# A fused scan and feed-forward kernel: the small scan products of the first two groups in fewer places, no filler products, one rounding step earlier

## The chip, the core and the metric

The kernel runs on one core of one Trainium2 chip. A core has TensorE (PE; its weight loads are shown as PEld), VectorE (DVE), ScalarE (ACT), GpSimd (POOL) and SyncE (SP, which here only issues transfers). Each works through its own queue in the order in which the program was written, and the engines wait for each other through semaphores. The metric is the device time of one execution in microseconds (us), less being better. The kernel before the change takes 375.94 us, the median of three runs (375.88 to 376.27). Its profile is of one more execution: 376.32 us by the same clock, and 374.6 us from the first to the last instruction, which is the span that all positions below count from.

## The reference

Two stages follow each other. The first is a Mamba-2 scan over 4 batches, 8 heads and 768 positions, head size 32, state size 16, cut into chunks. The reference uses chunks of 32; the result does not depend on the chunk.

```
la    = log(clip(a, 1e-6, 1));  cum = cumsum(la) within the chunk
M     = (C B^T) * exp(cum_i - cum_j) for i >= j, else 0
y     = M x  +  (C state) * exp(cum)
state = exp(sum la) * state + sum_j exp(cum_last - cum_j) B_j x_j
```

The second stage takes y as 3072 tokens of 256 numbers and computes `h = y w_in` (256x2048), `g = h * sigmoid(1.702 h)` and `g w_out` (2048x256). The weights come as 64-bit floats, and the kernel turns them into 32-bit ones on the chip.

## The kernel before, in words

**Tiling.** The kernel works with chunks of 128 positions. A batch has 6 chunks, so there are 24 in all, taken as 12 pairs (p = 0 to 11). A group is 512 tokens: two pairs, six groups (g = 0 to 5). For each group the scan of its two pairs gives yT, and the feed-forward follows in 8 blocks (j) of two hidden slices each.

**The scan of one pair** is a row of small products on TensorE, each of which uses the 128x128 array cut into strips: `turn_only` transposes B and C into one bank (tp), and ScalarE copies it out as BT and CT (L496). `gain` forms the state increments (A, L567, strips of 32 columns), and `keep` puts them into the state on VectorE. `score` forms C times B (cb, L539, strips of 32 rows), `weigh` multiplies it with the decay matrix L on VectorE (L550), and `since_start` scales C by the decay since the chunk's start (CsT, L524). `finish` forms y from state and L (L603, L612), and ScalarE copies the two halves of y into yT (L634). For the later pairs the decay matrix is made by a VectorE scan over broadcast rows of a (`decay`, L347). Pair 2 gets it from `fan_all`: four products (ab2, L355) spread rows of a over the array, and VectorE scans them (L382). `since_fanned` does the same for the decay since the start of the later chunks of batch 0, from two small products (L422 and L436).

**The start.** Pairs 0 and 1 are made from exponentials of differences. `mask` products (L447) preset the banks, `differ` adds the differences of the cumulated logarithms (L455), and ScalarE takes exponentials (L474). Ahead of `differ` stand one `keep_busy` product, six masks that are used, and two masks into a bank `idle` that nobody reads.

**The weights** come in ten pieces. For each, `fields` (L157, L160) splits the words on VectorE, `clamp` limits the exponent with two ScalarE instructions (L168, L169), `rounded` adds the low word (L173, VectorE), and `join` (L184, L190, VectorE) writes the piece into w_in or w_out. `narrow(i)` is `rounded(i)`, `fields(i+1)`, `join(i)`.

**The dense products.** Group 0 makes all its hidden slices first (`half`, `hidden`, L668 and L654) and then runs `project_all`, which accumulates 16 slices f into two banks (o, L766). Group 1 makes its hidden slices (steps H0 to H7) interleaved with the second product in a seven-product scheme (steps P0 to P7, `product`, L823). From group 2 on the first product uses a seven-product scheme too (`first`, L726 and L736). These schemes need mixed operands, which VectorE makes: `mix_in`, `mix_w`, `mix_y`, `mix_g`.

**What sets the order.** The order is written out by hand: tables `in_hidden`, `in_project` and `after` say what small work is put behind or ahead of which slice or step, and strings of steps do it for the later groups. At the end `in_order` fixes each engine's order as it was recorded. In `in_hidden[0]` the work stands behind slice f; in `in_project[0]` ahead of it; in `after` behind the named step.

**Banks.** Small results and hidden slices share a pool of four accumulation banks (`bank`, pool ps). An area of four more banks (`area`, pool psa) holds ab, cb or acc in turn. A tile of a pool waits until the last reader of the bank that it gets is done.

Of the kernel before, what the change touches and what calls it, by code (L numbers as in the profile page):

```python
# [16 lines left out]
P = 128  # L17
# [18 lines left out]
def kernel(  # L36
# [126 lines left out]
    def clamp(i):  # L163


        e = power[i]
        z = e.bitcast(FP32)
        nc.scalar.activation(z, e, AF.Relu, scale=-8.0, bias=edge[:, 0:1])  # L168
        nc.scalar.activation(e, z, AF.Relu, scale=-1.0, bias=edge[:, 1:2])  # L169
# [182 lines left out]
    def fan(p, r, ab):  # L352

        rows = slice(32 * r, 32 * r + 32)
        nc.tensor.matmul(out=ab, lhsT=ones[rows], rhs=fans[p][rows].rearrange("p k q i -> p (k q i)"),  # L355
                         start=True, stop=True, tile_position=(32 * r, 0),
                         skip_group_check=True)

    def fan_all(p):

        ab = area(f"ab{p}")
        for r in range(R):
            fan(p, r, ab[:, r])
        for r in range(R):
            decay_heads(p, r, ab[:, r])
        for k in range(2):
            ends(p, k)
# [51 lines left out]
    def fan_rows(t, c0, c1):  # L419

        o = bank(f"rows{c0}")[:, :(c1 - c0) * P]
        nc.tensor.matmul(out=o, lhsT=whose.rearrange("p h n -> p (h n)"),  # L422
                         rhs=t[:32, c0:c1].rearrange("p c s -> p (c s)"), start=True,
                         stop=True, tile_position=(0, 0), skip_group_check=True)
        return o
# [4 lines left out]
        nc.scalar.activation(since[0][:, :CG].rearrange("p c s -> p (c s)"),  # L430
                             fan_rows(cum, 0, CG), AF.Exp)

    def since_fanned():

        t, f = fan_rows(az, CG, NC), bank("starts")[:, :NC - CG]
        nc.tensor.matmul(out=f, lhsT=whose.rearrange("p h n -> p (h n)"),  # L436
                         rhs=starts[1][:32, CG:, 0], start=True, stop=True,
                         tile_position=(0, 0), skip_group_check=True)
        first = ssd.tile([P, NC, P], FP32, tag="first", name="first0", bufs=1)[:, CG:]
        nc.gpsimd.memset(first, 0.0)  # L440
        nc.vector.tensor_copy(first[:, :, 0], f)
        nc.vector.tensor_tensor_scan(
            out=since[0][:, CG:].rearrange("p c s -> p (c s)"), data0=t,
            data1=first.rearrange("p c s -> p (c s)"), initial=0.0, op0=ALU.mult, op1=ALU.add)

    def mask(t):
        nc.tensor.matmul(out=t, lhsT=identb, rhs=below.unsqueeze(1).to_broadcast([P, 4, P]),  # L447
                         start=True, stop=False, skip_group_check=True)
# [31 lines left out]
    def bank(name):  # L480
        return ps.tile([P, 4 * P], FP32, tag="ff", name=name)
# [448 lines left out]
    for r in range(2):  # L930
        ab[1, r] = bank(f"ab1_{r}")
        mask(ab[1, r])
    idle = bank("idle")
    for i in range(2):
        mask(idle)
    differ(0, [(r, ab[0, r]) for r in range(R)])
    exps(0, range(R))
    nc.vector.tensor_copy(idents, ident.unsqueeze(1).to_broadcast([P, NH, P]))
# [1 line left out]
    since_exp()  # L940
    fields(0)
    clamp(0)
    score(0, ab0)
    differ(1, [(r, ab[1, r]) for r in range(2)])
    exps(1, range(2))
# [1 line left out]
    ends(0, 0, nc.gpsimd)  # L947
    ends(0, 1, nc.gpsimd)
    weigh(0)
    rounded(0)  # L950
    turn_only(1, ("ACT", "ACT", "ACT"))
    gain(0)
    for r in range(2, R):
# [45 lines left out]
    at(in_hidden[0], 8, lambda: pick_a(PG))  # L999
    at(in_hidden[0], 9, lambda: clamp(6))  # L1000
    at(in_hidden[0], 9, lambda: fan_all(PG))
    at(in_hidden[0], 11, since_fanned, lambda: narrow(6))
    at(in_hidden[0], 15, lambda: clamp(7))
    for k in range(2):
        at(in_hidden[0], 5 + k, lambda k=k: spread(CG + 2 + k))
    at(in_hidden[0], 6, lambda: load(PG + 1))
    at(in_project[0], 0, lambda: turn_only(PG), lambda: narrow(7), lambda: since_start(PG))
    at(in_project[0], 1, lambda: advance(PG), lambda: clamp(8), lambda: decay(CG + 2))
    at(in_project[0], 4, lambda: scores(PG), lambda: narrow(8))
    at(in_project[0], 6, lambda: finish(PG), lambda: clamp(9), lambda: decay(CG + 3),  # L1010
       lambda: clip_rows(1), lambda: decay_rows(1))
    at(in_project[0], 7, lambda: turn(PG + 1))
    at(in_project[0], 9, lambda: narrow(9))
    at(in_project[0], 10, lambda: advance(PG + 1), lambda: scores(PG + 1))
    at(in_project[0], 14, lambda: finish(PG + 1))
    for i in range(4):
        at(in_project[0], 14, lambda i=i: mix_in(i))
    for k in range(PG):
# [3 lines left out]


    after = {}
    n, p = 2 * PG, 3 * PG

    def late(p):
        gain(p)
# [1 line left out]
        score(p)  # L1030
        weigh(p)

    at(after, "H0", lambda: decay(2 * CG), lambda: decay(2 * CG + 1), lambda: turn(n))
    at(after, "H1", lambda: late(n), lambda: decay(2 * CG + 2), lambda: decay(2 * CG + 3),
       lambda: turn(n + 1))
    at(after, "H3", lambda: finish(n), lambda: load(p + 1), lambda: late(n + 1))
    at(after, "H4", lambda: finish(n + 1))
    for k, i in enumerate(("H4", "P0", "P2", "P5")):
        at(after, i, lambda k=k: mix_w(k))
    for j in range(NF // 2):  # L1040
        at(after, f"P{min(j - 1, 5)}" if j else "H4", lambda j=j: mix_g(1, j))
    for k in range(CG):
        at(after, f"P{k}", lambda k=k: decay(3 * CG + k))
        at(after, "H1" if k < 2 else "H3", lambda k=k: spread(3 * CG + k))
    at(after, "P3", lambda: clip_rows(2), lambda: decay_rows(2), lambda: turn(p))
    at(after, "P4", lambda: mix_y(2), lambda: advance(p), lambda: turn(p + 1))
    at(after, "P5", lambda: advance(p + 1))
    assert [b for b in range(NB) if 3 * CG <= b * NC < 4 * CG] == [2]


# [7 lines left out]
    project_all(0, in_project[0])  # L1058
    load(p)
    spread_rows(2)  # L1060
    for step in "H0 H1 H2 H3 H4 P0 H5 P1 H6 P2 H7 P3 P4 P5".split():
        j = int(step[1:])
        if step[0] == "H":
            hidden(1, 2 * j)
            hidden(1, 2 * j + 1)
        else:
            product(1, j)
        for do in after.get(step, []):
            do()
# [14 lines left out]

    def seven(g, j):
        return [(g, j, (i,)) for i in ORDER]

    for g in range(2, NG):
        n, p = (g + 1) * PG, (g + 2) * PG
        more, most = g + 1 < NG, g + 2 < NG  # L1090
        chunks = list(range((g + 2) * CG, (g + 3) * CG)) if most else []
        rows = [b for b in range(NB) if most and (g + 2) * CG <= b * NC < (g + 3) * CG]
        if most:
            load(p)
            for c in chunks[:2]:
                spread(c)
            for b in rows:
                spread_rows(b)
        run(g, "0.1 P P 0.6 P P 0.7 P 0.5 P 0.2 P 0.D", seven(g - 1, 6))
        run(g, "1.1 0.S P 0.4 P P 1.6 P 0.3 0.T M P P 1.7 P 1.5 1.2 1.D C", seven(g - 1, 7),  # L1100
            M=lambda: mix_g(g, 0), C=lambda: combine(g - 1))
        def along():
            for r in rows:
                clip_rows(r)
                decay_rows(r)

        def refill():
            if most:
                load(p + 1)
                for c in chunks[2:]:  # L1110
                    spread(c)

        if more:

            run(g, "2.1 1.S 1.4 1.3 2.6 2.5 2.2 2.7 1.T s1 2.D 2.S w1 give 2.4 3.1 2.3 3.5 2.T 3.6 "
                "s2 w2 y1 refill 3.7 3.2 3.D along 4.1 P P 3.4 P 3.S 4.6 P 3.3 4.5 3.T M1 P P y2 4.7 P 4.2 4.D M2",
                seven(g, 0), s1=lambda: score(n), w1=lambda: weigh(n), give=lambda: give(g - 1),
                s2=lambda: score(n + 1), w2=lambda: weigh(n + 1), y1=lambda: finish(n),
                refill=refill, along=along, y2=lambda: finish(n + 1), M1=lambda: mix_g(g, 1),
                M2=lambda: mix_g(g, 2))  # L1120
            if most:
                decay(chunks[0])
        else:
            run(g, "2.1 1.S 1.4 1.3 2.6 2.5 2.2 2.7 1.T 2.D 3.1 2.S 2.4 3.5 3.6 2.3 3.2 3.7 2.T 3.D M",
                M=lambda: mix_g(g, 1))
        for j in range(5 if more else 4, NF // 2):
            h = "{1}.1 {0}.S P {0}.4 P {1}.6 P {0}.3 P {1}.7 {0}.T P {1}.5 P {1}.2 P {1}.D M".format(j - 1, j)
            run(g, h, seven(g, j - 4), M=lambda: mix_g(g, j - 2))
            if most:
                decay(chunks[j - 4])  # L1130
        k = NF // 2 - 1
        run(g, f"P {k}.S P {k}.4 P P {k}.3 {k}.T P P P", seven(g, 4))
        if not more:
            give(g - 1)
            for j in range(k - 1, k + 1):
                mix_g(g, j)
            break
        mix_g(g, 6)

        def ahead():  # L1140
            if most:
                for k in (p, p + 1):
                    turn_only(k)
                for k in (p, p + 1):
                    gain(k)
                for k in (p, p + 1):
                    since_start(k)
            mix_y(g + 1)
            if most:
                for k in (p, p + 1):  # L1150
                    keep(k)

        run(g, "P P A P P P P P", seven(g, 5), A=ahead)
        mix_g(g, 7)
    end(NG - 1, 5)

# [31 lines left out]
```

## Time and profile before

| what | before |
|---|---|
| time, median of 3 runs | 375.94 us (375.88 to 376.27) |
| span of the profiled execution | 374.6 us |
| TensorE / weight loads / VectorE / ScalarE busy | 98% / 76% / 71% / 41% |
| 0 to 24.25 us (start): TensorE, VectorE, ScalarE busy | 22.02, 17.39, 15.37 us |
| 24.25 to 52.30 us (hidden slices, group 0) | 28.05, 27.50, 18.38 us |
| 52.30 to 87.65 us (`project_all`) | 35.35, 32.88, 10.47 us |
| 87.65 to 142.85 us (group 1) | 55.20, 47.25, 15.22 us |
| 142.85 to the end | 226.81, 193.15, 142.50 us |
| transfers | 29.56 MB, mean 79 GB/s |

A busy share is the time in which an engine's records cover the span. The records of TensorE's matmuls overlap and their ends are modelled, so a full share does not say that the array works at its peak: the distance from one start to the next says more. A timeline line gives the start, the time covered, the engine, the line of the kernel, the operation, output and inputs by name, the array tile, the shape, and how many instructions were merged. A product of 32-bit numbers is two instructions (passes) in these lists, a transpose is one. A wait line gives who waited for whom, the total in us, how often, and the longest.

### The profile page before, as it was taken

To read this page: it belongs to the slowest core of one execution; us is meant where nothing else is said; L and a number is where in the kernel's file an instruction comes from. 1 tells how busy PE (TensorE), PEld (TensorE's weight loads), DVE (VectorE), ACT (ScalarE), POOL (GpSimd) and SP (SyncE) were. 2 spreads that over 40 slices of the span, in tenths; PEclk is the share of its full clock that TensorE was granted. 3 is DMA by queue.
4 is the path that set the end of the run, shared out by engine and by line. 5 is a ranking of instruction groups with operands and counts; after the bars stand their busy time and mean duration, and the time that the engine had idled before them with its cause. 6 is when DMAs were issued, how large, how long until landed. Compare 5 with 4: busy or idle time off the path is not lost.

```text
span 374.6 us, 5767 instructions
## 1 busy us (share of the span) xinstructions
PE 367.4 (98%) x2280; PEld 285.0 (76%) x2280; DVE 267.5 (71%) x439; ACT 152.3 (41%) x337; POOL 10.6 (3%) x34
## 2 busy tenths in 40 slices
PE   8999999999999999999999999999999999999995
PEld 3675457886457588788888878888878888888884
DVE  4899999999879967677887565888574355544343
ACT  4779552402421122453423544333454331554330
POOL 4200000100000010000000000000000000000000
PEclk9999999999999999999999999999999999999999
DMA  9997699615856110076300063000010000000011
GB/s 152 234 336 131 235 227 130 199 56 98 197 125 131 58 42 0 2 143 138 112 3 0 1 118 109 0 2 0 0 58 2 0 3 1 0 2 0 0 58 56
DMA packets 85794, 29.56 MB, mean 79 GB/s; under 512 B 75720, under 2 KB 79240, under 8 KB 85768
## 3 DMA queue, kind: packets, MB, share of 16 engines
q1 hardware_dynamic: 83320, 28.81, 32.6%
q10 hardware_dynamic: 2448, 0.39, 0.6%
q8 instruction: 18, 0.29, 0.3%
q14 instruction: 8, 0.07, 0.1%
HBM read 25.95 MB, written 3.24 MB: 78 GB/s over the span
## 4 chain that ended last, share of the span: by engine, by line
PE 94%; DVE 3%; ACT 1%; issue 1%; DVEq 0%; ACTq 0%
PE acc L823 32%; PE X L726 15%; PE h L654 13%; PE Y L736 11%; PE o L766 8%; PE cb L539 3%; PE y L612 3%; PE y L603 2%; PE h L668 1%; PE tp L491 1%; DVE L L550 1%; PE oT L857 1%; PE A L567 1%; PE ab L447 1%; PE ab L455 1%
## 5 line engine op out<-in xcount | busy, mean ns | idle before, releaser
L823 PE MATMUL acc<-mg,mw 128*128 128x256 f32 x240 | 65.3, 379 | 0.0
L731 ACT ACTIVATE ac<-X 128x256 f32<-128x256 f32 x64 | 24.6, 384 | 68.9 <-PE X L726 68.8
L823 PEld LDWEIGHTS acc<-mg,mw 128*128 128x128 f32 x240 | 45.6, 190 | 6.2
L654 PE MATMUL h<-yT,w_in 128*128 128x512 f32 x112 | 50.0, 595 | 0.0
L840 DVE TENSOR_TENSOR gT<-Y,ac 128x512 f32<-128x512 f32 x32 | 22.1, 692 | 38.8 <-PE Y L736 35.6
L703 ACT ACTIVATE gT<-gT 128x512 f32<-128x512 f32 x64 | 33.3, 520 | 28.5 <-DVE gT L840 28.5
L823 PE MATMUL acc<-gT,w_out 128*128 128x256 f32 x160 | 43.8, 380 | 0.0
L347 DVE TENSOR_TENSOR_SCAN L<-a,idents 128x1024 f32<-128x1024 f32 x18 | 41.1, 2283 | 0.0
L726 PE MATMUL X<-my,mi 128*128 128x256 f32 x128 | 38.7, 384 | 0.0
L654 PEld LDWEIGHTS h<-yT,w_in 128*128 128x128 f32 x112 | 20.8, 190 | 23.4 <-issue 22.4
L823 PEld LDWEIGHTS acc<-gT,w_out 128*128 128x128 f32 x160 | 30.1, 190 | 5.4 <-issue 1.4
L840 DVE TENSOR_TENSOR gT<-Y,b 128x256 f32<-128x256 f32 x32 | 13.5, 421 | 28.0 <-PE Y L736 27.7
L657 ACT ACTIVATE gT<-h 128x512 f32<-128x512 f32 x28 | 16.6, 595 | 39.6 <-PE h L654 39.5
L550 DVE TENSOR_TENSOR L<-L,cb 128x2048 f32<-128x2048 f32 (+1 forms) x12 | 25.3, 2108 | 5.7 <-PE cb L539 5.5
L766 PE MATMUL o<-w_out,gT 128*128 128x256 f32 x128 | 29.3, 383 | 0.0
L694 DVE TENSOR_TENSOR mg<-gT 128x512 f32<-128x512 f32 x40 | 27.3, 683 | 1.9 <-ACT gT L703 1.9
L726 PEld LDWEIGHTS X<-my,mi 128*128 128x128 f32 x128 | 23.8, 190 | 4.2 <-issue 1.2
L766 PEld LDWEIGHTS o<-w_out,gT 128*128 128x128 f32 x128 | 23.8, 190 | 4.1 <-issue 0.7
L823 PE MATMUL acc<-gT,mw 128*128 128x256 f32 (+1 forms) x86 | 24.0, 368 | 0.4 <-DVE c L840 0.4
L823 PE MATMUL acc<-mg,w_out 128*128 128x256 f32 x80 | 23.5, 379 | 0.0
L634 ACT ACTIVATE yT<-y 128x256 f32<-128x256 f32 x22 | 7.2, 381 | 35.8 <-PE y L612 35.5
L736 PE MATMUL Y<-yT,mi 128*128 128x256 f32 x64 | 19.4, 386 | 0.0
(145 smaller groups left out, 541.9 us busy)
## 6 DMA issues: line engine op xcount, KB each, us to landing
a<-scratch SPq DMA_DIRECT2D x18, 512.0 KB, 5.9
bits<-in_moe_w_out_dram SPq DMA_DIRECT2D x4, 1024.0 KB, 7.2
x<-in_x_dram SPq DMA_DIRECT2D x24, 128.0 KB, 3.3
out_dram<-ob SPq DMA_DIRECT2D x11, 256.0 KB, 2.4
bits<-in_moe_w_in_dram SPq DMA_DIRECT2D x4, 512.0 KB, 5.1
bits<-in_moe_w_in_dram SPq DMA_DIRECT2D x2, 1024.0 KB, 9.7
b<-in_B_dram SPq DMA_DIRECT2D x24, 64.0 KB, 3.7
c<-in_C_dram SPq DMA_DIRECT2D x22, 64.0 KB, 2.5
```

The costliest lines, as they stand in the source:

```text
L347: nc.vector.tensor_tensor_scan(out=Ls[p][:, k].rearrange("p r q i -> p (r q i)"), data0=ra[n], data1=idents.rearrange("p h i -> p (h i)"), ...
L550: nc.vector.tensor_tensor(out=Lv[:, k], in0=Lv[:, k], in1=cb.rearrange("p r k e -> p k r e")[:, k], op=ALU.mult)
L654: nc.tensor.matmul(out=h, lhsT=w_in[:, k, f * P:(f + 1) * P], rhs=yT[g][:, k], start=(k == 0), stop=(k == NK - 1))
L657: nc.scalar.activation(gT[g, j][:, i], h, AF.Silu, scale=GELU_SCALE)
L694: nc.vector.tensor_tensor(out=t[:, 0:2], in0=B[:, :, 1], in1=B[:, 0], op=ALU.subtract)
L703: nc.scalar.activation(o, i, AF.Silu, scale=GELU_SCALE)
L726: nc.tensor.matmul(out=s["X"], lhsT=lhsT, rhs=rhs, start=i == "1", stop=i == "4", skip_group_check=True)
L731: nc.scalar.activation(copy, s["X"], AF.Copy)
L736: nc.tensor.matmul(out=o, lhsT=lhsT, rhs=rhs, start=s.pop("new", False), stop=i != "5", skip_group_check=True)
L766: nc.tensor.matmul(out=o[k // 2][:, k % 2], lhsT=gT[g, f // 2][:, f % 2, k * P:(k + 1) * P], rhs=w_out[:, f], start=(f == 0 and k % 2 == 0 ...
L823: nc.tensor.matmul(out=acc[g][0][i][:, cols], lhsT=lhsT, rhs=rhs[:, cols], start=(j == 0 and i in (0, 2, 5, 6)), stop=(j == NF // 2 - 1), ...
L840: nc.vector.tensor_tensor(out=o, in0=v, in1=w, op=ALU.add)
```

## The change

It has four parts.

1. The two filler masks into `idle` are removed.
2. `rounded(0)`, one VectorE instruction, stands behind `clamp(0)` instead of behind `weigh(0)`.
3. In group 0 the small products are put together. The row and start products of `since_fanned` are issued by a new `fan_since`, right behind ab2, inside `fan_all`; `since_fanned` keeps the VectorE and GpSimd part. In `project_all`, `turn_only(2)`, `gain(2)` and `score(2)` stand together ahead of slice 1, where transposes stood ahead of slice 0, the increments ahead of slice 1 and the scores ahead of slice 4. `finish(2)` moves from slice 6 to slice 7, directly ahead of the transposes of pair 3. The transposes of pair 4 move from step H0 of group 1 to slice 14, directly behind `finish(3)`.
4. In group 1 the transposes and increments of pairs 6 and 7, which stood in steps P3 to P5, are issued together between the second and third product of block 5, by the function `ahead` that groups 2 to 4 already used. With it go `since_start` and `keep` of both pairs, `mix_y(2)`, and the places of `mix_w(3)`, `mix_g(1, 6)` and `mix_g(1, 7)`.

On TensorE this makes nine places where small products interrupt the dense ones in groups 0 and 1, instead of sixteen (transposes counted). No product but the two fillers is added or taken away, and the order of the transfers is the same.

```
-    idle = bank("idle")
-    for i in range(2):
-        mask(idle)
...
     clamp(0)
+    rounded(0)
     score(0, ab0)
...
     weigh(0)
-    rounded(0)
...
         for r in range(R):
             fan(p, r, ab[:, r])
+        fan_since()
...
-    at(in_hidden[0], 11, since_fanned, lambda: narrow(6))
+    at(in_hidden[0], 9, since_fanned)
+    at(in_hidden[0], 11, lambda: narrow(6))
...
-    at(in_project[0], 0, lambda: turn_only(PG), lambda: narrow(7), lambda: since_start(PG))
-    at(in_project[0], 1, lambda: advance(PG), lambda: clamp(8), lambda: decay(CG + 2))
-    at(in_project[0], 4, lambda: scores(PG), lambda: narrow(8))
-    at(in_project[0], 6, lambda: finish(PG), lambda: clamp(9), lambda: decay(CG + 3),
+    at(in_project[0], 0, lambda: narrow(7))
+    at(in_project[0], 1, lambda: turn_only(PG), lambda: gain(PG), lambda: score(PG),
+       lambda: since_start(PG), lambda: keep(PG), lambda: clamp(8), lambda: decay(CG + 2))
+    at(in_project[0], 4, lambda: weigh(PG), lambda: narrow(8))
+    at(in_project[0], 6, lambda: clamp(9), lambda: decay(CG + 3),
        lambda: clip_rows(1), lambda: decay_rows(1))
-    at(in_project[0], 7, lambda: turn(PG + 1))
+    at(in_project[0], 7, lambda: finish(PG), lambda: turn(PG + 1))
...
-    at(in_project[0], 14, lambda: finish(PG + 1))
+    at(in_project[0], 14, lambda: finish(PG + 1), lambda: turn_only(n))
...
-    at(after, "H0", lambda: decay(2 * CG), lambda: decay(2 * CG + 1), lambda: turn(n))
+    at(after, "H0", lambda: decay(2 * CG), lambda: decay(2 * CG + 1), lambda: since_start(n))
...
-    at(after, "P3", lambda: clip_rows(2), lambda: decay_rows(2), lambda: turn(p))
-    at(after, "P4", lambda: mix_y(2), lambda: advance(p), lambda: turn(p + 1))
-    at(after, "P5", lambda: advance(p + 1))
+    at(after, "P3", lambda: clip_rows(2), lambda: decay_rows(2))
...
+    run(1, "P P A P P P P P", seven(1, 5), A=lambda: ahead(2, p))
+    mix_g(1, 7)
```

In the changed kernel the lines of the score product, the transposes, the increments and ScalarE's copies are L546, L498, L574 and L503.

More of the change, by code (lines that the diff above doesn't have):

```diff
@@ L431, in since_exp, with fan_since @@
                              fan_rows(cum, 0, CG), AF.Exp)
-    def since_fanned():
-        t, f = fan_rows(az, CG, NC), bank("starts")[:, :NC - CG]
+    def fan_since():
+        t = fanned["rows"] = fan_rows(az, CG, NC)
+        f = fanned["starts"] = bank("starts")[:, :NC - CG]
         nc.tensor.matmul(out=f, lhsT=whose.rearrange("p h n -> p (h n)"),
@@ L438, in since_fanned @@
                          tile_position=(0, 0), skip_group_check=True)
+    fanned = {}
+    def since_fanned():
+        t, f = fanned["rows"], fanned["starts"]
         first = ssd.tile([P, NC, P], FP32, tag="first", name="first0", bufs=1)[:, CG:]
@@ L1006 @@
     at(in_hidden[0], 6, lambda: load(PG + 1))
-    at(in_project[0], 0, lambda: turn_only(PG), lambda: narrow(7), lambda: since_start(PG))
-    at(in_project[0], 1, lambda: advance(PG), lambda: clamp(8), lambda: decay(CG + 2))
-    at(in_project[0], 4, lambda: scores(PG), lambda: narrow(8))
-    at(in_project[0], 6, lambda: finish(PG), lambda: clamp(9), lambda: decay(CG + 3),
+    n, p = 2 * PG, 3 * PG
+    at(in_project[0], 0, lambda: narrow(7))
[3 more added lines that the diff above has]
+    at(in_project[0], 6, lambda: clamp(9), lambda: decay(CG + 3),
        lambda: clip_rows(1), lambda: decay_rows(1))
-    at(in_project[0], 7, lambda: turn(PG + 1))
+    at(in_project[0], 7, lambda: finish(PG), lambda: turn(PG + 1))
     at(in_project[0], 9, lambda: narrow(9))
     at(in_project[0], 10, lambda: advance(PG + 1), lambda: scores(PG + 1))
-    at(in_project[0], 14, lambda: finish(PG + 1))
+    at(in_project[0], 14, lambda: finish(PG + 1), lambda: turn_only(n))
     for i in range(4):
@@ L1024 @@
     after = {}
-    n, p = 2 * PG, 3 * PG
     def late(p):
@@ L1037 @@
     at(after, "H4", lambda: finish(n + 1))
-    for k, i in enumerate(("H4", "P0", "P2", "P5")):
+    for k, i in enumerate(("H4", "P0", "P2", "P4")):
         at(after, i, lambda k=k: mix_w(k))
     for j in range(NF // 2):
-        at(after, f"P{min(j - 1, 5)}" if j else "H4", lambda j=j: mix_g(1, j))
+        if j < 7:
+            at(after, f"P{min(j - 1, 4)}" if j else "H4", lambda j=j: mix_g(1, j))
     for k in range(CG):
@@ L1060 @@
     spread_rows(2)
-    for step in "H0 H1 H2 H3 H4 P0 H5 P1 H6 P2 H7 P3 P4 P5".split():
+    for step in "H0 H1 H2 H3 H4 P0 H5 P1 H6 P2 H7 P3 P4".split():
         j = int(step[1:])
@@ L1086, in seven, with ahead @@
         return [(g, j, (i,)) for i in ORDER]
+    def ahead(g, p=None):
+        pairs = (p, p + 1) if p else ()
+        for k in pairs:
+            turn_only(k)
+        for k in pairs:
+            gain(k)
+        for k in pairs:
+            since_start(k)
+        mix_y(g)
+        for k in pairs:
+            keep(k)
+    run(1, "P P A P P P P P", seven(1, 5), A=lambda: ahead(2, p))
+    mix_g(1, 7)
     for g in range(2, NG):
@@ L1138 @@
         mix_g(g, 6)
[L1140 to L1153, printed above, removed]
+        run(g, "P P A P P P P P", seven(g, 5), A=lambda: ahead(g + 1, p if most else None))
         mix_g(g, 7)
```

## The prediction

> **What bounds the kernel now.** I read the page first, then TensorE's waits, then the timelines of TensorE and ScalarE around each edited place.
>
> ```profile
> PE 367.4 (98%) x2280; PEld 285.0 (76%) x2280; DVE 267.5 (71%) x439; ACT 152.3 (41%) x337; POOL 10.6 (3%) x34
> ...
> PE 94%; DVE 3%; ACT 1%; issue 1%; DVEq 0%; ACTq 0%
> ```
>
> TensorE is busy for 98% of the span and is 94% of the chain that ended last: a microsecond put into or taken out of its stream after the start is a microsecond of the kernel. Next, what TensorE itself waited for, over the whole span:
>
> ```profile
> PE busy L373 <- DVE ones L256: 1.2, 1, 1.2
> PE ab L539 <- ACT L L474: 0.6, 1, 0.6
> PE h L668 <- DVE w_in L190: 0.4, 1, 0.4
> ...
> ```
>
> After the last of these (24.25 us) it runs without a listed wait until past 150 us, so all edits of the project stage and of group 1 lie on the path. The view of TensorE where the first edit of the project stage is made (start, time, engine, line, tiles, array tile, shape, count of passes; a 32-bit product is two passes, a transpose one):
>
> ```profile
> 52.31 0.38 PE L491 MATMUL tp<-ident,b 128*128 128x128 f32 x2
> ...
> 52.74 1.89 PE L766 MATMUL o<-w_out,gT 128*128 128x256 f32 x8
> 54.56 0.32 PE L567 MATMUL A<-x,Be 128*32 128x64 f32 x8
> 54.81 5.45 PE L766 MATMUL o<-w_out,gT 128*128 128x256 f32 x24
> 60.19 1.15 PE L539 MATMUL cb<-CT,BT 32*128 32x256 f32 x16
> ```
>
> Starts are to be subtracted, not durations. Six passes of a pure stretch (acc, from 113.88 to 115.17) take 1.295, 0.216 each. The eight o passes take 54.56-52.74=1.82 where 8x0.216=1.73: going into a small product costs 0.09. The 24 take 5.38 where 5.18 would do: 0.20, so coming out costs 0.11. Transposes cost 0.44 for four and nothing to go in or out. The other side of the same place, ScalarE:
>
> ```profile
> 52.51 0.60 ACT L657 ACTIVATE gT<-h 128x512 f32<-128x512 f32 x1 [1.12 <-PE h L654]
> 53.00 1.14 ACT L168 ACTIVATE p<-p,edge 128x1024 f32<-128x1024 uint32 x1
> 54.18 1.15 ACT L169 ACTIVATE p<-p,edge 128x1024 uint32<-128x1024 f32 x1
> 55.23 0.36 ACT L496 ACTIVATE BT<-tp 128x256 f32<-128x256 f32 x1
> 55.50 0.83 ACT L496 ACTIVATE CT<-tp,part 128x256 f32<-128x256 f32 x2
> ```
>
> tp2 was turned at 52.31, but its copies BT2 and CT2 ended only at 55.50+0.83=56.33, behind the two clamps of piece 7. The score product cb2 stood at 60.19, so this cost nothing. Last, the second half-scan, its eviction, and the model of a joined visit in group 2:
>
> ```profile
> 65.56 1.08 PE L612 MATMUL y<-L,x 128*32 128x128 f32 x32
> 66.58 1.99 PE L766 MATMUL o<-w_out,gT 128*128 128x256 f32 x8
> ```
>
> ```profile
> 66.49 0.66 ACT L634 ACTIVATE yT<-y 128x256 f32<-128x256 f32 x2 [7.95 <-PE y L612]
> ```
>
> ```profile
> 196.33 0.38 PE L491 MATMUL tp<-ident,b 128*128 128x128 f32 x2
> ...
> 197.30 0.54 PE L567 MATMUL A<-x,Be 128*32 128x64 f32 x24
> 197.77 0.70 PE L823 MATMUL acc<-gT,mw 128*128 128x256 f32 x2
> ```
>
> [...] BT2 starts at 55.23, as the second clamp ends. [...] the six masks from 3.12 to 5.63 take 0.42 each, a later pair (14.83 to 15.41) 0.29.
>
> **The change part by part.**
>
> *Fillers.* Two masks at 5.63 go. The first difference product starts at 6.62; the filler occupies the array until about then, while its operand, the first half of the scan (two halves from 5.67, 1.27 together), is done near 6.4. So at most 0.2 earlier[...]; all of the start up to 24.25 hangs on it. I take -0.1, bounds -0.2 and 0; the clock is a rival below.
>
> *Rounding.* L173, 0.68, moves from after L550 (12.44) to before it. VectorE is idle there for 0.91, waiting for the scores, so it fits. After L550 VectorE comes 0.3 earlier to the increments, but the next Be (18.57) waits for ScalarE's exponentials (17.45, 1.09 for two), which hang on TensorE. Worth 0: the piece's join has the slack.
>
> *Rows joined to the fan.* Row and start products (L422, L436) move from 44.59 to right behind ab2 (39.89). One exit and one entry go: the eight h passes between, 40.97 to 44.59, take 3.63, pure ones (115.60 to 119.04) 3.44. That is 0.20, and up to 0.1 more for ab2's tail. I take 0.25, so h ends at 52.22, not 52.47. The first output product then stands at its other operand, w_out of piece 6 (L190, 50.96+1.23=52.19, start 52.24).
>
> *tp2, A2, cb2 in one place.* TensorE: eight o passes from 52.24 to 53.97, four transposes to 54.41, entry 0.09, A2 to cb2 0.22 (as at 105.89 to 106.11): ready for cb2 at 54.72. But ScalarE still has the activation of the last h and both clamps ahead. Its chain runs from the end of h to the end of CT2, 52.47 to 56.33, 3.86 long; from 52.22 it ends at 56.08, and a product starts 0.05 after such an end. So TensorE waits from 54.72 to 56.13: 1.41. Then cb2 1.08, exit 0.11, 40 passes 8.63: 65.95. In the old order the same work is done at 64.92-0.09=64.83. Together +1.12 (the gains inside it -0.29). The transposes of the next pieces can't be pulled ahead: everything queued behind cb2 is output products, which wait too. VectorE's weighing and the joins behind it have slack: w_out of piece 7 is ready at 57.84, wanted near 62.
>
> *y2 with tp3, y3 with tp4.* The bank pool holds four. Two are the output sums, two are y; the transposes need a bank of y, so they wait for ScalarE's first y copy. It starts at 66.49; with 0.38 (of the pair's 0.66) it ends at 66.87, where the array was free at 66.58: a wait of 0.35. Going from y to transposes instead of o saves 0.05. +0.30, twice (the copies at 84.01 stand alike): +0.60. Piece 9's clamps, now ahead of y2's copies, end near 67.5, before y2 does near 69. b4 and c4 landed over 10 us earlier; SP's order is not changed.
>
> *tp6, tp7, A6, A7 together.* Before: A6 0.09+0.36, tp7's first pass 0.06 longer after it, A7 0.09+0.36+0.10: 1.07 beside the transposes. After, as in group 2: 0.09+(0.47 for 24 passes, 0.58 for 32)+0.10=0.77. -0.30. The sums mixed on VectorE change order (mw2, mg6 earlier, my2 later): my2 would be ready near 143, wanted at 144.2; the bank of X waits for CsT6, near 141, wanted at 142.6. Hidden, with at least 1.2 to spare.
>
> Sum: -0.1+1.12+0.60-0.30=+1.3. On the profiled span 374.6 gives 375.9. That execution ran at 376.32 in the list of times, 0.4 above the median, so I add to the median: 375.94+1.3=377.2.
>
> **Rivals.**
>
> *Faster.* ScalarE's copies don't hold the array: if CT2 and the y copies come before they are wanted, the waits (1.41+0.35+0.35=2.11) vanish and only the gains stay, -0.8: 375.1. For it: seven visits do go. Against: the clamps stand in the queue ahead of BT2. It decides when the three waits together come below 0.8.
>
> *No change.* A removed visit is worth twice what the gaps show. Then -0.8 becomes -1.6, net +0.5: 376.4. Against: the gaps of 0.09 and 0.11 repeat at every visit.
>
> *Much slower.* Without fillers the array is idle from about 5.7 to 6.4[...]: 1.4 in place of -0.1, 378.7. [...]
>
> That the change doesn't do what it says is out: the changed program's order has the nine visits.
>
> **How the numbers follow.** The forecast has 0.60, its own range 376.7 to 377.8; the faster rival 0.10; no change 0.17; the late clock 0.13. 0.2% is 0.75 us, about what a measurement of this kernel can tell from no change. Slower: 0.60 and 0.13, less 0.01; faster 0.10 and 0.02 of the third case; the rest, 0.16, within. The range leaves out 375.1 and the tail of the late clock: 376.1 to 378.6.
>
> **What would show it.** In the changed profile TensorE waits for ScalarE's CT (L503) once, about 1.4 near 55 us, and twice about 0.35 ahead of transposes (L498) near 69 and 86; A with 32 passes stands near 140 with one entry and exit; the first difference product starts near 6.4. Wrong if TensorE lists no wait at L546 in the project stage, or if the difference products take 3.5 instead of 2.2.

## The result, and the profile after

The changed kernel takes 377.42 us (median of 6 runs, 377.11 to 377.67) where the kernel before takes 375.99 (375.86 to 376.27): a ratio of 1.0037, 95% interval 1.0024 to 1.0050. It is slower by 1.43 us. The profiled execution of the changed kernel is its run of 377.11.

Its page first, the busy times and the shares of the chain that ended last:

```profile
PE 366.1 (98%) x2278; PEld 284.9 (76%) x2278; DVE 267.9 (71%) x439; ACT 152.4 (41%) x337; POOL 10.9 (3%) x34
...
PE 93%; ACT 2%; DVE 2%; DMA 1%; issue 0%; ACTq 0%; DVEq 0%
```

TensorE has 2 instructions fewer and is busy for 1.3 us less (366.1 after 367.4), yet the span is longer, 375.4 after 374.6. Of these 1.3 us, 1.0 lies in the start (22.02 and 21.05 up to the second block of hidden products), where the fillers went and whose length varies between executions; behind it TensorE is busy for 0.4 less (345.41 and 345.03) in a stretch that is 1.46 longer. So more was lost in waiting than was saved. TensorE's waits (line, what it waited for, total us, times, longest) name where:

```profile
PE busy L374 <- DVE ones L256: 1.2, 1, 1.2
PE cb L546 <- ACT CT L503: 1.1, 1, 1.1
PE tp L498 <- ACT yT L641: 0.6, 2, 0.3
...
```

The second and the third line are new; the first stood in before too, as L373. Of the lines further down one more is new, 0.3 us of the first difference products for VectorE's cum. It lies in the start, and is taken up with the fillers below. Now the place of tp2, A2 and cb2 on TensorE (start, time, engine, line, output and inputs, array tile, shape, passes; in brackets a wait and who ended it), from the last 24 passes of the hidden slices on:

```profile
40.82 10.73 PE L661 MATMUL h<-yT,w_in 128*128 128x512 f32 x24
51.66 1.97 PE L773 MATMUL o<-w_out,gT 128*128 128x256 f32 x8
53.47 0.38 PE L498 MATMUL tp<-ident,b 128*128 128x128 f32 x2
53.69 0.38 PE L498 MATMUL tp<-ident,c 128*128 128x128 f32 x2
54.00 0.32 PE L574 MATMUL A<-x,Be 128*32 128x64 f32 x8
55.45 1.15 PE L546 MATMUL cb<-CT,BT 32*128 32x256 f32 x16 [1.14 <-ACT CT L503]
```

and the same stretch on ScalarE:

```profile
51.59 0.60 ACT L664 ACTIVATE gT<-h 128x512 f32<-128x512 f32 x1 [1.12 <-PE h L661]
52.08 1.14 ACT L168 ACTIVATE p<-p,edge 128x1024 f32<-128x1024 uint32 x1
53.25 1.15 ACT L169 ACTIVATE p<-p,edge 128x1024 uint32<-128x1024 f32 x1
54.31 0.36 ACT L503 ACTIVATE BT<-tp 128x256 f32<-128x256 f32 x1
54.57 0.83 ACT L503 ACTIVATE CT<-tp,part 128x256 f32<-128x256 f32 x2
```

From the start of A2 to that of cb2 it is 55.45-54.00=1.45, and A2 itself needs 0.25 (54.56 to 54.81 in before): the array stands for 1.21 (1.457 less 0.249 before rounding). The profile has 1.14 for this wait, since it counts from A2's modelled end, and the expectations below write 1.23 for it. CT2 ends at 54.57+0.83=55.40, and cb2 starts 0.05 later. No product starts between A2's last pass and cb2: the output products that stand behind cb2 come at 56.53, after it. The wait at y2, on TensorE and then on ScalarE:

```profile
67.73 1.08 PE L619 MATMUL y<-L,x 128*32 128x128 f32 x32
69.10 0.44 PE L498 MATMUL tp<-ident,b 128*128 128x128 f32 x2 [0.29 <-ACT yT L641]
```

```profile
68.66 0.66 ACT L641 ACTIVATE yT<-y 128x256 f32<-128x256 f32 x2 [1.99 <-PE y L619]
```

The transposes start 1.37 after the first pass of y, which needs 1.01 in before: a wait of 0.36 until the first of the two copies (68.66 and some 0.38) is done. y3 shows the same 1.37. Last, the joined place at the end of group 1:

```profile
140.88 0.65 PE L574 MATMUL A<-x,Be 128*32 128x64 f32 x32
141.47 0.70 PE L830 MATMUL acc<-gT,mw 128*128 128x256 f32 x2
```

The four pairs of transposes stand just ahead of the 32 passes of A, which take 141.47-140.88=0.59 with the exit. The small products are entered and left once, and no new wait is listed behind them.

To sum up without the start, whose length differs between profiled executions, as shown below, I use one **section**: from the first hidden product with the second block of weights (24.25 in before, 23.57 in after) to the end of the span. Before takes 350.37 in it, after 351.83: +1.46, where the medians differ by 1.43. By place, as differences of starts: rows joined to the fan -0.25; the place of tp2, A2 and cb2 +1.36 (wait 1.21, a new wait for w_out 0.35, one entry and exit fewer -0.20); tp3 behind y2 +0.31 and tp4 behind y3 +0.31; end of group 1 -0.29. That is +1.44.

### The profile page after: what moved, and what is told of

The parts are those of the page before. It is cut to its first block, busy times and chain, and to the rows that moved or that the text cites. A ratio compares the mean times of both kernels' runs of the same rounds, so it can differ in the third digit from the quotient of the medians.

```text
span 375.4 us, 5762 instructions
## 1 busy us (share of the span) xinstructions
PE 366.1 (98%) x2278; PEld 284.9 (76%) x2278; DVE 267.9 (71%) x439; ACT 152.4 (41%) x337; POOL 10.9 (3%) x34
## 4 chain that ended last, share of the span: by engine, by line
PE 93%; ACT 2%; DVE 2%; DMA 1%; issue 0%; ACTq 0%; DVEq 0%
PE acc L830 32%; PE X L733 15%; PE h L661 13%; PE Y L743 11%; PE o L773 7%; PE cb L546 3%; PE y L619 3%; PE y L610 2%; PE ab L462 1%; PE h L675 1%; PE tp L498 1%; PE oT L864 1%; ACT L L481 1%; DMA az<-in_a_dram 1%; PE A L574 1%; DVE L L557 1%
```

## The experiments

All of them compute everything that the reference asks for. The time of each is a median; before was measured beside each at 375.82 to 375.88. The section is read from one profiled execution of each kernel; where two kernels are the same from there on, it agrees within 0.02 (before and e1, after and e7), so it carries the verdicts. The medians are coarser: their distance from before differs from the section's by up to 0.2. The medians of e1, e6, e8 and e11 lie below what was expected, by 0.01 to 0.18, and that of e5 above; before itself, measured beside them, came some 0.1 lower than the 375.94 that the expectations start from.

| kernel | us | ratio to before, 95% | section us |
|---|---|---|---|
| before | 375.99 | | 350.37 |
| after | 377.42 | 1.0037 (1.0024 to 1.0050) | 351.83 |
| e1: before, start edits alone | 375.69 | 0.9999 (0.9991 to 1.0007) | 350.36 |
| e2: before, end of group 1 alone | 375.41 | 0.9992 (0.9985 to 0.9998) | 350.07 |
| e8: before, rows alone | 375.47 | 0.9992 (0.9984 to 1.0000) | 350.10 |
| e7: after, fillers back | 377.33 | 1.0041 (1.0028 to 1.0054) | 351.81 |
| e3: after, tp3 and tp4 a slice later | 376.62 | 1.0021 (1.0013 to 1.0029) | 351.18 |
| e4: after, cb2 three slices later | 376.17 | 1.0007 (0.9999 to 1.0015) | 350.78 |
| e5: after, clamps of piece 7 earlier | 377.12 | 1.0034 (1.0022 to 1.0047) | 351.65 |
| e9: after, tp2 earlier | 377.20 | 1.0043 (1.0027 to 1.0058) | 351.82 |
| e10: after, clamps of piece 7 behind | 377.10 | 1.0031 (1.0019 to 1.0042) | 351.63 |
| e11: after, e9 and e10 together | 375.58 | 0.9992 (0.9983 to 1.0000) | 350.25 |
| e6: after, no waits | 374.99 | 0.9978 (0.9971 to 0.9985) | 349.62 |

**The start alone (e1).** The edits to before:

```diff
-    idle = bank("idle")
-    for i in range(2):
-        mask(idle)
...
     clamp(0)
+    rounded(0)
     score(0, ab0)
...
     weigh(0)
-    rounded(0)
```

> The kernel before with the two edits of the start alone: the two filler masks are gone and the first piece's rounding stands ahead of its first weighing; everything else as before. Theory of the prediction (ScalarE's copies hold the array later, the start is worth about nothing): 375.9, between 375.7 and 376.0. Rival, the late clock[...]: 377.4, that is the whole loss of the change. From the first hidden product with the second block of weights to the end both theories expect what before took, 350.4.

The ratio is 0.9999; its interval holds a gain of 0.1 as well as none. The section is 0.01 from that of before, as it must be, since the edits lie ahead of it. The late clock (a start 1.4 longer without the fillers, an estimate of the author's) is out: the kernel without them is no slower.

**Fillers put back (e7).** The edit to after:

```diff
+    idle = bank("idle")
+    for i in range(2):
+        mask(idle)
     differ(0, [(r, ab[0, r]) for r in range(R)])
```

> The changed kernel with the two filler masks put back at the start. Theory (the fillers are worth about nothing): 377.3 to 377.5, as the changed kernel. Rival, the late clock: 376.0, the fillers buy more than 1.

377.33, the changed kernel within its interval. The profiled starts say the same. The section begins with fillers at 24.25 (before), 23.76 (e2), 23.68 (e8) and 23.48 us (e7), without them at 23.76 (e1), 23.57 (after), 23.56 (e3), 23.89 (e4) and 23.48 to 23.85 (e5, e6, e9, e10 and e11). The new wait for cum is no mark of the missing fillers either: e2, which has them, lists it with 0.7. The late start in the profile of before is the scatter of single executions, and not the fillers.

**The end of group 1 alone (e2).** The core of the edits to before (the mixing steps that stood at P5 move as in the change):

```diff
-    at(after, "P3", lambda: clip_rows(2), lambda: decay_rows(2), lambda: turn(p))
-    at(after, "P4", lambda: mix_y(2), lambda: advance(p), lambda: turn(p + 1))
-    at(after, "P5", lambda: advance(p + 1))
+    at(after, "P3", lambda: clip_rows(2), lambda: decay_rows(2))
...
+    run(1, "P P A P P P P P", seven(1, 5), A=lambda: ahead(2, p))
+    mix_g(1, 7)
```

> The kernel before with the joining at the end of group 1 alone (tp6, tp7, A6, A7 in one place). Theory: two entries and exits fewer, -0.3: 375.7, and 350.1 from the first hidden product with the second block of weights to the end. Rival 'a visit is worth twice its gaps': -0.6, 375.4. Rival 'the changed order of the sums on VectorE brings a new wait for X or for the activations of piece 2': 376.0 or more, with a wait of TensorE near 142 to 145 that before does not list.

The section falls by 0.30, and TensorE lists no wait between 139 and 150 us. The gain is the gaps counted once: "worth twice" asked for 0.6. The medians could not decide this: 375.41 is 0.47 below the 375.88 of before, and the interval of the ratio runs from 0.1 to 0.6 us.

**The rows alone (e8).** The core of the edits to before (since_fanned then takes the two products as given):

```diff
+        fan_since()
         for r in range(R):
             decay_heads(p, r, ab[:, r])
...
-    at(in_hidden[0], 11, since_fanned, lambda: narrow(6))
+    at(in_hidden[0], 9, since_fanned)
+    at(in_hidden[0], 11, lambda: narrow(6))
```

> The kernel before with the joining of the rows alone: the products for the rows and their starts stand right behind the sums ab2, and the scan over them on VectorE two steps earlier. Theory of the prediction: -0.25, 375.65, with the first output product waiting for the weights w_out of piece 6 on VectorE. Reading of the changed kernel's trace: two visit gaps and 0.1 of ab2's tail go (-0.4 in all), but 0.16 is given back at a hidden product waiting for VectorE's first0 and up to 0.28 at the first output product: -0.1 to -0.25, 375.65 to 375.8. Rival 'VectorE gives all of it back': 375.9 or more.

The section falls by 0.26. Of the gaps that go, 0.15 is given back among the 24 hidden passes behind: they take 10.56, where 0.53 for the first and 23 of 0.43 would be 10.4. No wait is listed for it, but one of these passes starts at 46.22, right after VectorE's copy of the starts (L448, 46.01+0.15), 0.05 later than the pace, and the next takes 0.53. With tp2 still ahead of the output products (0.44 of transposes), the weights w_out are ready when the first of these comes; in the changed kernel they aren't. There the same 24 passes and the way to the first output product take 51.66-40.82=10.84, 0.28 more, and the array waits this long for VectorE's

```profile
50.29 1.23 DVE L190 SCALAR_TENSOR_TENSOR w_out<-m,p 128x1024 f32<-128x1024 f32 x1
```

which ends at 51.52; the product follows 0.15 later, as it does in every kernel here that has tp2 behind the output products. The first pass after it takes 0.07 longer than behind transposes. This is the 0.35 of the sum above: it belongs to the move of tp2, not to the rows, and it is gone in e9, which puts tp2 back.

**The bank waits (e3).** The edit to after:

```diff
-    at(in_project[0], 7, lambda: finish(PG), lambda: turn(PG + 1))
+    at(in_project[0], 7, lambda: finish(PG))
+    at(in_project[0], 8, lambda: turn(PG + 1))
...
-    at(in_project[0], 14, lambda: finish(PG + 1), lambda: turn_only(n))
+    at(in_project[0], 14, lambda: finish(PG + 1))
+    at(in_project[0], 15, lambda: turn_only(n))
```

> The changed kernel with the transposes of tp3 and tp4 one slice of output products later than y2 and y3, instead of right behind them. Theory: the two waits for ScalarE's first y copy (0.35 each) vanish, and 0.05 each comes back since y is followed by output products again: -0.6 against the changed kernel, 376.8, and 351.2 from the first hidden product with the second block of weights to the end. Rival 'the bank waits are listed but cost nothing, since the array would lose the time at the next place anyway': 377.4, no difference.

The section falls by 0.64 and the two waits for yT leave TensorE's list. So they cost what they show, and eight output passes between y and the transposes (1.83 in before, 66.58 to 68.41) are enough to hide the copy.

**The score product later (e4).** The edit to after:

```diff
-    at(in_project[0], 1, lambda: turn_only(PG), lambda: gain(PG), lambda: score(PG),
+    at(in_project[0], 1, lambda: turn_only(PG), lambda: gain(PG),
...
-    at(in_project[0], 4, lambda: weigh(PG), lambda: narrow(8))
+    at(in_project[0], 4, lambda: score(PG), lambda: weigh(PG), lambda: narrow(8))
```

> The changed kernel with the score product cb2 taken out of the place with A2 and put three slices later, just ahead of the weighing. Theory: the wait of TensorE for ScalarE's copies of C (1.23 measured in the changed kernel) is gone, one entry and exit (0.2) comes back: -1.0, 376.4, and 350.8 from the first hidden product with the second block of weights to the end. Rival 'a visit is worth twice its gaps': -0.8, 376.6. Rival 'the wait only moves, to another of ScalarE's copies or to the weights of the output': -0.3 or less, 377.1 or more, with a new wait of TensorE between 54 and 66.

The section falls by 1.05, of which 1.02 up to the start of y2: the wait of 1.21 gone, one entry and exit of 0.19 back. No wait takes its place. The wait for CT2 is thus the largest part of the loss.

**Why CT2 is late (e5, e9, e10, e11).** The prediction put the two clamps of piece 7 down as the cause. The first try moved them ahead of the last activations:

```diff
-    at(in_hidden[0], 15, lambda: clamp(7))
+    at(in_hidden[0], 13, lambda: clamp(7))
```

> The changed kernel with the two clamps of piece 7 on ScalarE put two steps of the hidden stage earlier, so that they no longer stand ahead of the copies of B and C that the score product cb2 waits for. Theory (the wait is ScalarE's queue[...]): ScalarE then goes from the last activation straight to the copies, whose chain is 0.6+0.3+0.8; the wait in the place of A2 and cb2 falls from 1.23 to between 0.2 and 0.8, the kernel is 0.4 to 1.0 faster than the changed one: 376.7 (376.3 to 377.0). Rival 'the wait is for the transposes or for the table of part, whatever ScalarE does': 377.3, wait unchanged. Rival 'the clamps then hold the activations of the last hidden products': 377.0 or more, with a new wait of TensorE at L661 or at the first output product.

The wait fell only from 1.21 to 1.02, and the section by 0.17, which was outside what I expected. ScalarE now stood idle ahead of the copies:

```profile
54.41 0.38 ACT L503 ACTIVATE BT<-tp 128x256 f32<-128x256 f32 x1 [1.95 <-PE tp L498]
54.69 0.83 ACT L503 ACTIVATE CT<-tp,part 128x256 f32<-128x256 f32 x2
```

It waited for the transposes themselves. The clamps also held an activation, but this cost nothing that shows: the hidden passes keep their pace, and the first output product waits 0.31, where it waited 0.28 in after, and starts again 0.15 behind w_out (51.82 to 51.97). So it is the same wait for w_out, and not the sign of the rival of the held activations. (The view of the weight loads names the activation as what ended it, but that was done 0.09 before w_out.) So the theory was amended: two things each hold the copies back to about the same moment, the clamps, and the transposes that were moved behind eight output passes. Three kernels take away one, the other, and both. e9, an edit to after:

```diff
-    at(in_project[0], 0, lambda: narrow(7))
-    at(in_project[0], 1, lambda: turn_only(PG), lambda: gain(PG), lambda: score(PG),
+    at(in_project[0], 0, lambda: turn_only(PG), lambda: narrow(7))
+    at(in_project[0], 1, lambda: gain(PG), lambda: score(PG),
```

> The changed kernel with the transposes tp2 alone put back ahead of the first output products; ScalarE's queue is left as in the changed kernel (clamps of piece 7 ahead of the copies). Theory now: two things each hold the copies back to about the same moment, the late transposes and the two clamps; taking one away is worth nearly nothing. The copy of C still ends behind the clamps near 55.4, so cb2 starts where it did, TensorE only waits longer for it (1.5 in place of 1.2): 377.3, at most 0.1 better than the changed kernel. Rival 'the transposes alone are the cause': the wait is gone, 376.0 to 376.2.

e10, an edit to after; e11 is e9's edit and this one:

```diff
-    at(in_hidden[0], 15, lambda: clamp(7))
...
-    at(in_project[0], 0, lambda: narrow(7))
+    at(in_project[0], 0, lambda: rounded(7), lambda: fields(8))
+    at(in_project[0], 2, lambda: join(7))
...
-       lambda: since_start(PG), lambda: keep(PG), lambda: clamp(8), lambda: decay(CG + 2))
+       lambda: since_start(PG), lambda: keep(PG), lambda: clamp(7), lambda: decay(CG + 2))
+    at(in_project[0], 2, lambda: clamp(8))
```

> The changed kernel with the two clamps of piece 7 alone put behind the copies of the place with A2 and cb2 (and the join of piece 7's weights on VectorE two slices later, behind them); the transposes stay in that place. Theory now: the copies can't start before the transposes are done, so the wait falls from 1.2 to 1.0 only, as in the kernel with the clamps early, but no hidden product waits: 377.2, 0.2 better than the changed kernel. Rival 'the clamps alone are the cause', as the prediction put it: the wait falls to 0.2 to 0.5, 376.5 or less.

> Both of these edits in the changed kernel: transposes tp2 ahead of the first output products, and the clamps of piece 7 behind the copies. Theory now: the copies of B and C start near 52.2 and end near 53.3, cb2 follows A2 at 53.9 without a wait, 1.5 earlier than in the changed kernel: 375.9 (375.7 to 376.1). The three kernels together: 0.1 and 0.2 alone, 1.5 together. Rival 'the join of piece 7, two slices later, makes the output products wait for their weights': 376.3 or more, with a wait of TensorE for w_out near 62.

Against the changed kernel the section falls by 0.01 in e9, 0.20 in e10 and 1.57 in e11. In e9 the copies still come behind both clamps: these start at 51.98 and 53.15, BT2 at 54.21. TensorE's wait in e9, where it only grew, and in e10:

```profile
PE cb L546 <- ACT CT L503: 1.5, 1, 1.5
```

```profile
PE cb L546 <- ACT CT L503: 1.0, 1, 1.0
```

ScalarE in e10, where the transposes alone hold the copies:

```profile
54.12 0.38 ACT L503 ACTIVATE BT<-tp 128x256 f32<-128x256 f32 x1 [1.92 <-PE tp L498]
54.40 0.83 ACT L503 ACTIVATE CT<-tp,part 128x256 f32<-128x256 f32 x2
```

and in e11, where neither does:

```profile
51.53 0.60 ACT L664 ACTIVATE gT<-h 128x512 f32<-128x512 f32 x1 [1.12 <-PE h L661]
52.02 0.38 ACT L503 ACTIVATE BT<-tp 128x256 f32<-128x256 f32 x1
52.28 0.84 ACT L503 ACTIVATE CT<-tp,part 128x256 f32<-128x256 f32 x2
```

There the copies follow the last activation at once, CT2 is done at 53.12 and cb2 starts at 53.83, right behind A2:

```profile
53.59 0.32 PE L574 MATMUL A<-x,Be 128*32 128x64 f32 x8
53.83 1.15 PE L546 MATMUL cb<-CT,BT 32*128 32x256 f32 x16
```

Taking away either cause alone was worth 0.2 or less; both together 1.57. In the section e11 is even 0.12 below before: the gains of the rows, the visit and the end of group 1 are there, and only the two waits for yT are left of the losses.

**No waits at all (e6).** Edits to after, beside those of e3:

```diff
-    at(in_project[0], 0, lambda: narrow(7))
-    at(in_project[0], 1, lambda: turn_only(PG), lambda: gain(PG), lambda: score(PG),
-       lambda: since_start(PG), lambda: keep(PG), lambda: clamp(8), lambda: decay(CG + 2))
-    at(in_project[0], 4, lambda: weigh(PG), lambda: narrow(8))
+    at(in_project[0], 0, lambda: turn_only(PG), lambda: narrow(7), lambda: since_start(PG))
+    at(in_project[0], 1, lambda: clamp(8), lambda: decay(CG + 2))
+    at(in_project[0], 4, lambda: gain(PG), lambda: score(PG), lambda: keep(PG), lambda: weigh(PG), lambda: narrow(8))
```

> The changed kernel with all three waits taken away at once: tp2 stands ahead of the output products as in before, its A2 and cb2 stand together four slices later, and tp3 and tp4 one slice behind y2 and y3. The joining of the rows, the start and the end of group 1 stay as in the changed kernel. Theory: only the gains of the change stay, rows -0.2, one visit -0.2, group 1's end -0.3, start -0.1 to 0: 375.15 (375.0 to 375.3), faster than before by 0.7 to 0.8. Rival 'a joined visit is worth nothing, or the rows' gain is eaten by VectorE's later weights of the output': 375.5 to 375.7. Rival 'a visit is worth twice its gaps': 374.5.

374.99, and the section is 0.75 below that of before: rows 0.25, one visit 0.20, end of group 1 0.30. This is the version that beats both kernels. Its place of A2 and cb2 shows how: tp2 first, then 32 output passes during which ScalarE does its clamps and copies, then both small products without a wait.

```profile
51.72 7.07 PE L773 MATMUL o<-w_out,gT 128*128 128x256 f32 x32
58.72 0.32 PE L574 MATMUL A<-x,Be 128*32 128x64 f32 x8
58.97 1.15 PE L546 MATMUL cb<-CT,BT 32*128 32x256 f32 x16
```

## Why the prediction was right, point by point

The sum was +1.3, and the measured change +1.43. Behind the start the parts add up to +1.42 as predicted and to +1.44 by place.

**Start, -0.1 predicted.** Nothing that can be seen: e1 and e7 can't be told from the kernels they were made from, so neither -0.1 nor 0 is shown, and the rounding step has no run of its own. The predicted sign, a first difference product near 6.4, tells nothing: it starts at 6.14 in after, and at 6.11 in e7, with the fillers. The late clock did not come: the 32 difference products took 2.01 in after (6.14 to 8.15) and 2.19 in before (6.62 to 8.81). Its 3.5 for them and its 1.4 for the kernel were the author's estimates, with no trace behind them.

**Rows, -0.25.** -0.25 in after, -0.26 alone in e8.

**tp2, A2 and cb2, +1.12 with the rows.** +1.11. The start of cb2 was met: ab2 starts 0.67 earlier in this execution (39.22, in before 39.89), so the predicted 56.13 is 55.46 here, and it was 55.45. The wait ahead of it was mis-sized, 1.21 and not 1.41, because the array came to it later: the first output product lost 0.35 to w_out (0.28 of waiting, 0.07 at its first pass), where the predicted start at 52.24 held 0.18 (52.31 less the 0.25 of the rows is 52.06). The prediction took 0.05 from the end of w_out to the product, and it was 0.15. As cb2 waits for CT2 anyway, this cost nothing by itself; the two are one loss of 1.56, which e11 took away as a whole (1.57).

**Its cause.** The step "ScalarE still has the activation of the last h and both clamps ahead" is true of the changed kernel, but it told half. The same copies would have been nearly as late without the clamps, since the transposes had been moved behind eight output passes; e10 shows that this alone leaves 1.0 of the wait, e11 that both have to go to remove it. The time came out right because the clamps, which the sum used, are the later of the two, by 0.2. The rival "faster" was argued against with the clamps alone; each of the two causes is enough against it.

**tp3 and tp4, +0.30 each.** +0.31 each, and -0.64 for both when taken away in e3. The reason given, a bank freed by ScalarE's first y copy, is what the trace names as releaser.

**End of group 1, -0.30.** -0.29 in after, -0.30 alone in e2. The changed order of the sums on VectorE brought no wait.

**Rivals.** "A visit is worth twice its gaps" is out: e2 gives the gaps of two visits once (0.30), and e4 pays one entry and exit once (1.21 less 1.02 is 0.19).

## What to carry to other kernels

Putting small products together saves an entry and an exit, 0.2 us here, only if what the later one reads has had its time; between a transpose and the product that reads its copy lies a way over another engine (in e10, where ScalarE was free, 55.28-54.01=1.27 us from A2, right behind the transposes, to cb2), and this distance in other work must be kept when the steps are joined. The same goes for a buffer that a copy must free first (0.31 lost at y2 and at y3 each). And when the removal of a suspected cause changes nothing, look at what now holds the same instruction: two causes that end at nearly the same moment show little singly (0.01 and 0.20 here, 1.57 together), and only the kernel without both tells.

## What the runs showed of the hardware that I had not expected

The time up to the second block of hidden products differs by 0.8 us between profiled executions (23.48 to 24.25), with and without fillers; the second half of the first difference products begins at 7.85 in before, at 7.18 in after, and at 7.08 in e7, which has the fillers. Part of it is the pace of TensorE itself: the six masks ahead of the fillers, the same instructions in both kernels, take 2.51 in before (3.12 to 5.63), 0.42 each, and 1.99 in e2 (3.11 to 5.10), 0.33 each. So two single profiles can differ at the start by more than half of the effect sought here, while from the second block on, e1 repeats before and e7 repeats after within 0.02 in 350 us.
